# Interleaved linear and softmax attention on one core: squares of VectorE's exponentials go to GpSimd, and the passage between the attentions is reordered

## The chip, the cores and the metric

The kernel runs on one core of one Trainium2 chip, as one launch. The metric is the device time of that launch in microseconds (us); lower is better. The engines are named as the profile names them: PE (TensorE, matrix products), ACT (ScalarE), DVE (VectorE), POOL (GpSimd), and SP (SyncE), which issues the transfers.

## The reference

Two blocks, A and B, are applied in turn, A, B, A, B, to x of shape 1 x 2048 x 1024 (32 heads of 32), each behind a layer norm and with a residual addition.

```python
def _A_ref(x, wqkv, w_phi, wo):          # linear attention
    q, k, v = split_heads(x @ wqkv)
    pq, pk = q @ w_phi, k @ w_phi        # per head
    phi_q = concat(softmax(pq), softmax(-pq))
    phi_k = concat(softmax(pk), softmax(-pk))
    kv, z = phi_k^T @ v, sum(phi_k)
    o = (phi_q @ kv) / (phi_q @ z + 1e-6)
    return merge_heads(o) @ wo

def _B_ref(x, wqkv, wo):                 # softmax attention
    q, k, v = split_heads(x @ wqkv)
    p = softmax(q @ k^T * 32 ** -0.5)
    return merge_heads(p @ v) @ wo

x = x + _A_ref(layernorm(x)); x = x + _B_ref(layernorm(x))
x = x + _A_ref(layernorm(x)); x = x + _B_ref(layernorm(x))
```

## The kernel before

x stays in SBUF as `xR` (16 row tiles of 128 x 1024). Four chunks of 512 rows are worked on. A "layer" is one A block and the B block behind it, so there are two. For each, the A block's keys and values are made chunk by chunk (`a_keys`), summed into a state (`a_state`), and read by the queries (`a_queries`, `a_out`); then comes the softmax attention (`attention`), whose output projection (`b_out`) adds into `xR`. In the first layer, the next layer's norms and keys of chunks 0 to 2 are made beside the attention; only those of chunk 3 have to wait for its end.

Nothing is issued in the order in which it is written. The functions record operations with a planned length, a priority and buffers. `Sched.run` then plays a model of the five engines, takes the ready operation of lowest priority number on each, grants buffers, and writes the instructions in the order it finds. Each engine on the chip runs its instructions strictly in that order and waits for semaphores where data or buffers are not there yet. All SBUF buffers come from one arena of 162 KB per partition; PSUM's eight banks are granted by class, with quotas (`QUOTA`).

**The attention.** A unit is 128 keys x 512 queries of one head: 2048 units a layer. PE makes the scores of up to three units into one half of banks 0 to 5 (L1148), ACT takes the exponential of all of them in one instruction (L1208), and PE multiplies the result by the values and by ones into bank 6 (L1337), which DVE copies out (L1353). Bank 7 is for the projections that run beside it (L544, in four column groups), whose results DVE copies out (L994, L1006, L1022). DVE also computes some exponentials itself (`exp_dve`), of units `spare` picks some 34 units ahead, two to a `pair`. L1290 clamps the scores from PSUM to SBUF as fp32 `y` (class `xy`, two buffers in the tile `work`); then follows a chain on `y` and on `x` (class `xx`, one buffer in `work`). In the first layer each unit goes through by itself (128 x 512):

- mask the mantissa of `y` into `x` (L1111), mask the exponent of `y` (L1114);
- `v`: y = (x + R) * y (L1098);
- `h`: x = (x + B) * x (L1098), the square;
- last: e = (x + C) * y, to bf16 in the arena (L1098).

In the second layer both units of a pair go together (128 x 1024), and the result comes as two bf16 factors whose products are summed by PE:

```python
m = ts(... scalar1=0x007FFFFF, scalar2=0x3F000000 ...)   # L1102: mask y into x
a = ts(... scalar1=0x7F80, scalar2=EXP2S_D ...)          # L1105: high half of y to e2
h = stt(x_v, x_v, EXP2S_B, x_v, a, [x_b])                # L1098: x = (x + B) * x
done.append(stt(e_v, x_v, EXP2S_C, y_v, h, [x_b, y_b, e_b], 0.12))
```

All of the chain is on DVE. POOL only makes constants, clears (L836, L1409) and one small cast per key tile (L779).

**The end of the first attention.** `b_out` multiplies the last chunk's outputs by the projection in two steps: six eighths early, into `part`, the last two when the last heads are there (banks `TAIL`). Eight additions (L1062), two for each row tile, write `xR`. `ln_rows` then does the statistics (L580, L583), ACT the root (L598, L601), DVE the scaling (L607), PE the transposition (L617), ACT the copy (L620), and the key products begin (L540).

**Dummy products.** While an attention is open, `Sched.run` puts a product into a throw-away bank (`idle`, `idle_acc`) where the model shows PE with less than `KEEP` = 0.75 of the last 3.4 us at work. Outside of the attentions there are none.

Of the kernel before, what the change touches and what calls it, by code (L numbers as in the profile page):

```python
# [21 lines left out]
C512 = 512  # L22

# [37 lines left out]
class Sched:  # L61
    def __init__(self, sbuf_bytes, quota):
        self.ops = []
        self.quota = quota
        self.live = {}
        self.free = [(0, sbuf_bytes)]
        self.bank_used = [False] * 11
# [128 lines left out]
    def run(self):  # L196
# [21 lines left out]
        accum = False  # L218
        started = {}
        for o in self.ops:  # L220
            if o.ndep == 0:
                heapq.heappush(ready[o.eng], (0 if o.first else 2, o.prio, o.seq, o))
        t, left, order = 0.0, len(self.ops), []
        while left:
            moved = False
            for e in engines:
                if busy[e] > t + 1e-9 or not ready[e]:
                    continue
# [23 lines left out]
                for s in skipped:  # L252
                    heapq.heappush(ready[e], s)
                if pick is None and e == "PE" and self.idle is not None and self.live.get("S", 0):
# [19 lines left out]
                if pick.hook is not None:  # L274
                    pick.hook(pick)
                    left += self.more
                    self.more = 0
                if e == "PE":
                    recent.append((t, t + pick.dur))
                    if pick.accum is not None:  # L280
                        accum = pick.accum
                d = pick.dur
                if pick.mode is not None:
# [45 lines left out]

SBUF_ARENA = 162 * 1024  # L330
WIDE = 3
# [4 lines left out]
MODEST = {"slabk", "xn1", "e1", "vp1", "pkf", "wo", "bo"}  # L336
QUOTA = {"pk": 3, "pv": 3, "kv": 1, "mm": 4, "cmp": 5, "bc": 6, "num": 1, "wt": 5, "wx": 2, "fil": 3,
         "e": 6, "vp": 6, "e1": 4, "vp1": 4, "E": 10, "q2": 4, "kt": 4, "w2": 5, "oT": 27, "T": 4, "den": 2,
         "eq": 8, "ns": 4, "cw": 6, "hl": 6, "oc": 2, "slab": 12, "slabk": 3, "fin": 4,
         "rs": 8, "pkf": 1, "cden": 2, "part": 8, "w2r": 1,  # L340
         "wo": 1, "st": 4, "xo": 6, "bn": 4, "xs": 1, "xy": 5, "xx": 1, "E1": 5}
CORE = {"E", "E1", "T", "den", "cden", "oT"}
E_SIZE = 3 * 1024
HOLES = 3
SPELL = 3.4
KEEP = 0.75

ONE = 2.0**23
# [55 lines left out]
WIRE = 360.0  # L404
BACKLOG = 1.0
KV_MM = 0.042


@with_exitstack
def kernel(  # L410
# [59 lines left out]
    arena = arena_p.tile([P, ARENA // 2], BF16, tag="arena")  # L470
    work = const.tile([P, 3, 2 * C512], F32, tag="work")
    psum = psum_p.tile([P, 8 * C512], F32, tag="psum")
# [523 lines left out]
    def soon(o):  # L996
        o.first = True
        return o
# [49 lines left out]

    def b_out(t, fc, c, prio, w, oT, banks, last, part=None, lo=0, hi=4):

        wb, ww, wd = w
        pb, pv = ps("fil", banks)
        ts = slice(t * P, (t + 1) * P)
# [7 lines left out]
        def add(out_, in0, deps, bufs):  # L1061
            return soon(op("DVE", dve_us(512), lambda: nc.vector.tensor_tensor(  # L1062
                out=out_(), in0=in0(), in1=pv(), op=ALU.add), [m, *deps], [pb, *bufs], prio))
        x_v = lambda: xR[:, row, fs]
# [17 lines left out]
    def exp_dve(pair, prio, each):  # L1082

        n = len(pair["got"])
        y_b, e_b = pair["bufs"]
        x_b, x = fixed("xx", [(10,)])
        sch.enter(x_b, prio)
        done = []
        for lo, hi in [(k, k + 1) for k in range(n)] if each else [(0, n)]:
# [7 lines left out]
            def stt(out_, in0, scalar, in1, dep, bufs, us=0.0):  # L1097
                return sch.later("DVE", dve_us(w * 512) + us, lambda: nc.vector.scalar_tensor_tensor(  # L1098
                    out=out_(), in0=in0(), scalar=scalar, in1=in1(), op0=ALU.add, op1=ALU.mult), [dep], bufs, prio)
            got = done[-1:] + pair["got"][lo:hi]  # L1100
            if pair["split"]:
                m = ts(lambda y_v=y_v, x_v=x_v: nc.vector.tensor_scalar(  # L1102
# [19 lines left out]
    def attention(base, kT, vT, q_of, gate, most, mix, turns, pos, split, ahead, near, load, each):  # L1122

# [130 lines left out]
        def spare(rows, turn, more):  # L1254
# [10 lines left out]
            if pair is None:  # L1265
                y_b, y_v = fixed("xy", [(8,), (9,)])
                e_b, e_v = sb("E1", 4 if split else 2, C512)
                new += [y_b, e_b]
# [6 lines left out]
            if pair is None:  # L1275
                state["pair"] = {"split": split, "got": [], "units": [], "y": y_v, "e": e_v, "bufs": (y_b, e_b),
                                 "flat": lambda: e_v().rearrange("p a b -> p (a b)")}
                for b in (y_b, e_b):
                    b.left += 1
# [147 lines left out]
    for layer in range(2):  # L1427
# [87 lines left out]
        oTs = attention(at, kT, vT, q_of, gate, MOST[layer], MIX[layer], turns, pos, SPLIT[layer], AHEAD[layer], NEAR[layer], LOAD[layer], EACH[layer])  # L1515
        if last:
# [28 lines left out]
        for i in range(G):  # L1545
# [63 lines left out]
```

## Time and profile before

| what | us |
|---|---|
| median of 3 runs | 2268.9 (2268.39 to 2270.06) |
| the profiled execution | 2269.66 |
| its span, first to last instruction | 2267.9 |
| PE busy | 2192.6 |
| ACT busy | 1997.2 |
| DVE busy | 1892.7 |
| POOL busy | 26.9 |

The span is what lies between the first and the last instruction; the execution's own time is 1.8 us longer. A busy PE is not PE at its peak, since matrix products are pipelined and their ends are modelled. A row of a group gives line, engine, operation, out<-in, shapes and count, then busy us and mean ns, then idle us before it and what ended that. A row of a timeline gives start and length in us.

### The profile page before, as it was taken

How to read it: one execution, taken by the hardware profiler on the slowest of the kernel's cores; microseconds unless marked ns; L12 is line 12 of the kernel's file. 1: busy time of each engine (PE TensorE's matmuls, PEld its weight loads, DVE VectorE, ACT ScalarE, POOL GpSimd, SP SyncE). 2: the span in 40 equal slices, each digit the busy share in tenths (PEclk: the TensorE clock that was granted, in tenths of full speed). 3: DMA queues.
4: the chain of work that ended last, by engine and by line, in shares of the span. 5: the costliest groups of instructions: out<-in, count | busy, mean ns of one | idle time of the engine just before them, and what ended most of it. 6: DMA issues, size and time to landing. Idle time of an engine off the chain costs nothing.

```text
span 2267.9 us, 65202 instructions
## 1 busy us (share of the span) xinstructions
PE 2192.6 (97%) x28080; PEld 823.7 (36%) x28080; DVE 1892.7 (83%) x3015; ACT 1997.2 (88%) x1970; POOL 26.9 (1%) x78
## 2 busy tenths in 40 slices
PE   9999999999999999999998999999999999999998
PEld 5543443333333333333333444443333333333332
DVE  8866536999899999999897686357999899899997
ACT  6447669999999999999896644899999999999998
POOL 1000000000000000000000000000000000000000
PEclk9999999999999999999999999999999999999999
DMA  8701221111223314314344013111111111121111
GB/s 234 202 5 38 71 59 28 44 48 47 61 77 90 100 54 120 89 54 132 114 118 124 1 38 100 36 35 29 40 39 38 44 37 38 37 73 51 46 30 35
DMA packets 235193, 150.56 MB, mean 66 GB/s; under 512 B 131608, under 2 KB 211480, under 8 KB 234904
## 3 DMA queue, kind: packets, MB, share of 16 engines
q1 hardware_dynamic: 234904, 146.40, 23.4%
q8 instruction: 219, 3.59, 0.6%
q14 instruction: 70, 0.57, 0.1%
HBM read 81.59 MB, written 27.77 MB: 48 GB/s over the span
## 4 chain that ended last, share of the span: by engine, by line
PE 51%; ACT 30%; DVE 9%; issue 7%; DMA 2%; SPq 1%; ACTq 0%; POOL 0%; DVEq 0%; POOLq 0%
ACT arena L1208 27%; PE psum L540 14%; PE psum L544 14%; PE psum L1337 11%; PE psum L1148 9%; DVE work L1098 1%; DVE work L1290 1%; DVE arena L1098 1%; DMA arena<-in_B_wo_dram 1%; DVE arena L953 1%; DMA arena<-rd 1%; DVE arena L765 1%; PE psum L796 1%; DVE xR L968 1%; ACT arena L935 1%
## 5 line engine op out<-in xcount | busy, mean ns | idle before, releaser
L1208 ACT ACTIVATE arena<-psum 128x1536 bf16<-128x1536 f32 (+1 forms) x1337 | 1673.0, 1422 | 13.2 <-PE psum L1148 11.2
L1337 PE MATMUL psum<-arena 128*32 128x512 bf16 x4328 | 663.3, 383 | 2.5 <-DVE arena L1353 2.1
L1337 PE MATMUL psum<-arena,ones_bf 128*32 128x512 bf16 x4328 | 663.9, 383 | 1.7 <-issue 1.7
L544 PE MATMUL psum<-arena 128*32 128x512 bf16 (+1 forms) x8768 | 613.6, 377 | 8.7 <-DVE arena L757 2.0
L1148 PE MATMUL psum<-arena 32*128 32x512 bf16 x4096 | 523.6, 384 | 42.4 <-ACT arena L1208 36.7
L540 PE MATMUL psum<-arena 128*128 128x512 bf16 (+1 forms) x2032 | 451.0, 374 | 4.6 <-DVE arena L1374 2.2
L1098 DVE SCALAR_TENSOR_TENSOR work<-work 128x512 f32<-128x512 f32 (+1 forms) x456 | 374.8, 822 | 8.1
L1148 PEld LDWEIGHTS <-arena 32*128 32x128 bf16 x4096 | 153.9, 91 | 579.4 <-issue 571.7
L1290 DVE TENSOR_SCALAR work<-psum 128x512 int32<-128x512 f32 x402 | 275.3, 686 | 62.7 <-PE psum L1148 58.9
L544 PEld LDWEIGHTS <-arena 128*32 128x32 bf16 x8768 | 197.5, 96 | 253.5 <-issue 145.3
L540 PEld LDWEIGHTS <-arena 128*128 128x128 bf16 x2032 | 192.6, 98 | 231.1 <-issue 23.2
L1337 PEld LDWEIGHTS <-arena 128*32 128x32 bf16 x4328 | 186.3, 95 | 237.4 <-issue 156.1
L1098 DVE SCALAR_TENSOR_TENSOR arena<-work 128x512 bf16<-128x512 f32 (+1 forms) x286 | 257.3, 900 | 4.9
L1337 PEld LDWEIGHTS <-ones_bf 128*32 128x32 bf16 x4328 | 185.3, 95 | 30.2 <-issue 8.8
L994 DVE CAST arena<-psum 128x512 bf16<-128x512 f32 (+1 forms) x104 | 67.2, 646 | 55.4 <-PE psum L544 54.7
L761 ACT ACTIVATE arena<-psum 128x512 bf16<-128x512 f32 x80 | 43.4, 594 | 73.0 <-PE psum L540 64.0
L893 ACT ACTIVATE arena<-psum 128x512 bf16<-128x512 f32 x128 | 70.7, 597 | 40.0 <-PE psum L540 37.6
L765 DVE TENSOR_REDUCE arena<-arena 128x32 f32<-128x1024 bf16 x64 | 77.8, 1215 | 21.1 <-ACT arena L761 19.3
L1353 DVE COPY arena<-psum 128x512 f32<-128x512 f32 x126 | 86.0, 683 | 9.5 <-PE psum L1337 9.3
L544 PE MATMUL psum<-xR,onesD 128*32 128x512 bf16 x1148 | 89.7, 380 | 0.4 <-DVE work L1290 0.2
L1102 DVE TENSOR_SCALAR work<-work 128x1024 int32<-128x1024 int32 x116 | 79.9, 689 | 2.6
L774 DVE TENSOR_TENSOR arena<-psum,arena 128x1024 bf16<-128x1024 f32 x64 | 77.5, 1212 | 4.2 <-DVE arena L768 0.2
(98 smaller groups left out, 1272.4 us busy)
## 6 DMA issues: line engine op xcount, KB each, us to landing
arena<-rd SPq DMA_DIRECT2D x62, 256.0 KB
arena<-in_B_wqkv_dram SPq DMA_DIRECT2D x51, 256.0 KB
xa<-arena SPq DMA_DIRECT2D x48, 256.0 KB
arena<-in_A_wqkv_dram SPq DMA_DIRECT2D x40, 256.0 KB
arena<-in_B_wo_dram SPq DMA_DIRECT2D x40, 256.0 KB
arena<-arena SPq DMA_DIRECT2D x256, 32.0 KB
arena<-wd_k SPq DMA_DIRECT2D x32, 256.0 KB
arena<-arena SPq DMA_DIRECT2D x62, 128.0 KB
```

The lines of the kernel that those rows point to most:

```text
L540: nc.tensor.matmul(out_, lhsT=lhsT, rhs=rhs, start=start, stop=stop, skip_group_check=True)
L544: nc.tensor.matmul(out_[ks, :], lhsT=lhsT[:, ks], rhs=rhs, start=start, stop=stop, tile_position=(0, 32 * k), skip_group_check=True)
L765: red = op("DVE", dve_us(1024), lambda ev=ev, sv=sv: nc.vector.reduce_sum(out=sv(), in_=ev().rearrange("p s (h d) -> p (s h) d", d=DH), ax ...
L774: ml = op("DVE", dve_us(1024), lambda vpv=vpv, wv_=wv_, sv=sv: nc.vector.tensor_tensor(out=wv_()[:, :, :, 0:DH], in0=vpv().rearrange("p (h ...
L893: ex = [op("ACT", act_us(512), lambda s=s, pv=pv, ev=ev: nc.scalar.activation(out=ev()[:, s, :], in_=pv(), func=ACT.Exp, scale=(1.0, -1.0) ...
L1098: return sch.later("DVE", dve_us(w * 512) + us, lambda: nc.vector.scalar_tensor_tensor(out=out_(), in0=in0(), scalar=scalar, in1=in1(), op ...
L1102: m = ts(lambda y_v=y_v, x_v=x_v: nc.vector.tensor_scalar(out=x_v().bitcast(I32), in0=y_v().bitcast(I32), scalar1=0x007FFFFF, scalar2=0x3F ...
L1148: nc.tensor.matmul(out=out_, lhsT=kT[g][1]()[r, pp, d * P:(d + 1) * P], rhs=q_of[(qc, g)][1]()[r, (pp + j // 2) % 2, :], start=True, stop= ...
L1208: ex = make("ACT", act_us(w * C512), lambda: nc.scalar.activation(out=e_v()[:, 0:w * C512], in_=s_v()[:, 0:w * C512], func=ACT.Exp, scale= ...
L1290: pair["got"].append(sch.later("DVE", dve_us(512) + 0.13, lambda: nc.vector.tensor_scalar(out=y_v().bitcast(I32)[:, k, :], in0=s_v(), scal ...
L1337: nc.tensor.matmul(out=a_v()[col:col + 32, :], lhsT=v_v()[:, kc % 4, o:o + DH] if what == 0 else ones_bf[:], rhs=ev()[:, x * C512:(x + 1) ...
L1353: cp = op("DVE", dve_us(512), lambda t_v=t_v, a_v=a_v: nc.vector.tensor_copy(out=t_v(), in_=a_v()), [last], [a_b, t_b], prio - 4)
```

## The change

1. The square goes to POOL in both layers (`HALF_POOL`), as two instructions in place: x = x + B/2, then x = x * x. The last step's constant takes up the difference. In the second layer POOL is released by L1102's mask, in the first by `v`; the last step on DVE waits for POOL. `x` gets a second buffer (`XS`), for which the arena gives up 4 KB per partition. The scheduler's model is told `POOL_NS` = 2.87 ns per element for the product and 0.9 for the shift.
2. The last chunk's additions in the first layer get the priority of the norm that reads them, tile by tile, instead of coming ahead of everything; the tail products get a class of banks of their own (`tl`).
3. Outside of the attentions, behind the first 40 us of the model, dummy products (`idle_at`) are put into a free bank where the model shows PE at work for less than 0.95 of the last 3.4 us. The model now also counts a product at double length for 4 us after PE was idle for 2.1 of the last 3.4 us.

```diff
+YS, XS = 2, 2
...
+                if pick is None and e == "PE" and self.idle is not None and not self.live.get("S", 0) and t > WARM_UP:
+                    recent = [r for r in recent if r[1] > t - SPELL]
+                    spot = next((x for x in (7, 5, 4, 3, 2, 1, 0) if not self.bank_used[x]), None)
+                    if sum(not x for x in self.bank_used[:8]) > 1 and sum(r[1] - max(r[0], t - SPELL) for r in recent) < KEEP_N * SPELL:
+                        pick = Op("PE", MM, 0.0, lambda spot=spot: self.idle_at(spot), (Buf("ps", 0, "idle", [(spot,)]),), 0.0, "n", 0)
...
+                    if t > WARM_UP and sum(r[1] - max(r[0], t - SPELL) for r in recent) < SPELL - REST:
+                        slow = t + DIP
+                    if t < slow:
+                        d *= 2
...
-SBUF_ARENA = 162 * 1024
+SBUF_ARENA = (162 - 4 * (YS + XS - 3)) * 1024
...
+KEEP_N = 0.95
+REST = 2.1
+DIP = 4.0
+WARM_UP = 40.0
...
+POOL_NS = 2.87
+HALF_POOL = (True, True)
...
-        pb, pv = ps("fil", banks)
+        pb, pv = ps("tl" if banks is TAIL else "fil", banks)
...
-            return soon(op("DVE", dve_us(512), lambda: nc.vector.tensor_tensor(
-                out=out_(), in0=in0(), in1=pv(), op=ALU.add), [m, *deps], [pb, *bufs], prio))
+            o = op("DVE", dve_us(512), lambda: nc.vector.tensor_tensor(
+                out=out_(), in0=in0(), in1=pv(), op=ALU.add), [m, *deps], [pb, *bufs], prio if add_at is None else add_at)
+            return o if add_at is not None else soon(o)
...
-        x_b, x = fixed("xx", [(10,)])
+        x_b, x = fixed("xx", [(8 + YS + i,) for i in range(XS)])
...
+            def square(scalar, dep):
+                if not pair["pool"]:
+                    return stt(x_v, x_v, scalar, x_v, dep, [x_b])
+                sh = sch.later("POOL", w * C512 * 0.9 / 1000 + 0.1, lambda x_v=x_v: nc.gpsimd.tensor_scalar(
+                    out=x_v(), in0=x_v(), scalar1=scalar / 2, scalar2=None, op0=ALU.add), [dep], [x_b], prio)
+                return sch.later("POOL", w * C512 * POOL_NS / 1000 + 0.1, lambda x_v=x_v: nc.gpsimd.tensor_tensor(
+                    out=x_v(), in0=x_v(), in1=x_v(), op=ALU.mult), [sh], [x_b], prio)
...
-                h = stt(x_v, x_v, EXP2S_B, x_v, a, [x_b])
-                done.append(stt(e_v, x_v, EXP2S_C, y_v, h, [x_b, y_b, e_b], 0.12))
+                h = square(EXP2S_B, m if pair["pool"] else a)
+                done.append(stt(e_v, x_v, EXP2S_C - (EXP2S_B**2 / 4 if pair["pool"] else 0.0), y_v, [h, a], [x_b, y_b, e_b], 0.12))
...
-            h = stt(x_v, x_v, EXP2_B, x_v, v, [x_b])
-            done.append(stt(e_v, x_v, EXP2_C, y_v, h, [x_b, y_b, e_b], 0.12))
+            h = square(EXP2_B, v)
+            done.append(stt(e_v, x_v, EXP2_C - (EXP2_B**2 / 4 if pair["pool"] else 0.0), y_v, h, [x_b, y_b, e_b], 0.12))
...
-                new[qc][t].append(b_out(t, fc, qc, pr, w, oTs[qc], TAIL, last, part, 3, 4))
+                new[qc][t].append(b_out(t, fc, qc, pr, w, oTs[qc], TAIL, last, part, 3, 4,
+                                        BASE[1] + 10 * qc - LA + 0.01 * t - 0.005))
...
+    def idle_at(x):
+        nc.tensor.matmul(psum[:, x * C512:(x + 1) * C512], lhsT=onesD[:], rhs=xR[:, 0, 0:C512], start=True, stop=True)
+    sch.idle_at = idle_at
```

More of the change, by code (lines that the diff above doesn't have):

```diff
@@ L66, in __init__ @@
         self.free = [(0, sbuf_bytes)]
-        self.bank_used = [False] * 11
+        self.bank_used = [False] * 14
         self.peak = 0
@@ L219, in run @@
         started = {}
+        slow = 0.0
         for o in self.ops:
@@ L226, in run @@
             for e in engines:
-                if busy[e] > t + 1e-9 or not ready[e]:
+                if busy[e] > t + 1e-9 or not ready[e] and (e != "PE" or t < WARM_UP):
                     continue
@@ L253, in run @@
                     heapq.heappush(ready[e], s)
+                if pick is None and e == "PE" and self.idle is not None and not self.live.get("S", 0) and t > WARM_UP:
[3 more added lines that the diff above has]
+                        pick = Op("PE", MM, 0.0, lambda spot=spot: self.idle_at(spot), (Buf("ps", 0, "idle", [(spot,)]),), 0.0, "n", 0)
+                        pick.bufs[0].left, pick.late = 1, True
+                        self.queue["idle"] = [list(pick.bufs), 0]
+                        assert self._alloc(pick.bufs)
+                        left += 1
                 if pick is None and e == "PE" and self.idle is not None and self.live.get("S", 0):
@@ L470 @@
     arena = arena_p.tile([P, ARENA // 2], BF16, tag="arena")
-    work = const.tile([P, 3, 2 * C512], F32, tag="work")
+    work = const.tile([P, YS + XS, 2 * C512], F32, tag="work")
     psum = psum_p.tile([P, 8 * C512], F32, tag="psum")
@@ L1047, in b_v, with b_out @@
             done[(t, h)] = e
-    def b_out(t, fc, c, prio, w, oT, banks, last, part=None, lo=0, hi=4):
+    def b_out(t, fc, c, prio, w, oT, banks, last, part=None, lo=0, hi=4, add_at=None):
         wb, ww, wd = w
-        pb, pv = ps("fil", banks)
+        pb, pv = ps("tl" if banks is TAIL else "fil", banks)
         ts = slice(t * P, (t + 1) * P)
@@ L1098, in stt @@
                 return sch.later("DVE", dve_us(w * 512) + us, lambda: nc.vector.scalar_tensor_tensor(
-                    out=out_(), in0=in0(), scalar=scalar, in1=in1(), op0=ALU.add, op1=ALU.mult), [dep], bufs, prio)
+                    out=out_(), in0=in0(), scalar=scalar, in1=in1(), op0=ALU.add, op1=ALU.mult), dep if isinstance(dep, list) else [dep], bufs, prio)
             got = done[-1:] + pair["got"][lo:hi]
+            def square(scalar, dep):
[5 more added lines that the diff above has]
+                    out=x_v(), in0=x_v(), in1=x_v(), op=ALU.mult), [sh], [x_b], prio)
             if pair["split"]:
@@ L1117, in exp_dve, with attention @@
             v = stt(y_v, x_v, EXP2_R, y_v, a, [x_b, y_b])
-            h = stt(x_v, x_v, EXP2_B, x_v, v, [x_b])
-            done.append(stt(e_v, x_v, EXP2_C, y_v, h, [x_b, y_b, e_b], 0.12))
+            h = square(EXP2_B, v)
+            done.append(stt(e_v, x_v, EXP2_C - (EXP2_B**2 / 4 if pair["pool"] else 0.0), y_v, h, [x_b, y_b, e_b], 0.12))
         return done
-    def attention(base, kT, vT, q_of, gate, most, mix, turns, pos, split, ahead, near, load, each):
+    def attention(base, kT, vT, q_of, gate, most, mix, turns, pos, split, ahead, near, load, each, pool):
         units = [
@@ L1265, in spare @@
             if pair is None:
-                y_b, y_v = fixed("xy", [(8,), (9,)])
+                y_b, y_v = fixed("xy", [(8 + i,) for i in range(YS)])
                 e_b, e_v = sb("E1", 4 if split else 2, C512)
@@ L1275, in spare @@
             if pair is None:
-                state["pair"] = {"split": split, "got": [], "units": [], "y": y_v, "e": e_v, "bufs": (y_b, e_b),
+                state["pair"] = {"split": split, "pool": pool, "got": [], "units": [], "y": y_v, "e": e_v, "bufs": (y_b, e_b),
                                  "flat": lambda: e_v().rearrange("p a b -> p (a b)")}
@@ L1514 @@
                     q_of[(qc, g)] = q_back(g, qc, at + 10 * pos[(qc, g)] - QB, away)
-        oTs = attention(at, kT, vT, q_of, gate, MOST[layer], MIX[layer], turns, pos, SPLIT[layer], AHEAD[layer], NEAR[layer], LOAD[layer], EACH[layer])
+        oTs = attention(at, kT, vT, q_of, gate, MOST[layer], MIX[layer], turns, pos, SPLIT[layer], AHEAD[layer], NEAR[layer], LOAD[layer], EACH[layer], HALF_POOL[layer])
         if last:
```

9 lines of the change are left out of this document (5 added, 4 removed).

## The prediction

> **What bounds the kernel now.** I read the page first, then busy time by stage, then the groups with their shapes kept apart.
>
> ```profile
> PE 2192.6 (97%) x28080; PEld 823.7 (36%) x28080; DVE 1892.7 (83%) x3015; ACT 1997.2 (88%) x1970; POOL 26.9 (1%) x78
> ```
>
> The shares mix stages, so I asked for busy time in four stretches: the first layer's attention, the passage to the second layer, the projections after it, the second layer's attention. Columns: stretch, length, then busy time of PE, PEld, DVE, ACT, POOL, granted clock, DMA share, GB/s.
>
> ```profile
> 350.00:1216.00 866.00, 830.65 (x12370) 286.82 (x12371) 805.04 (x1401) 855.77 (x715) 9.99 (x25) 0.99 0.29 81
> 1216.00:1236.00 20.00, 14.22 (x101) 6.75 (x94) 14.00 (x27) 7.21 (x16) 0.00 (x0) 0.83 0.53 172
> 1236.00:1444.00 208.00, 206.50 (x1506) 93.53 (x1508) 140.16 (x240) 108.62 (x199) 2.59 (x8) 1.00 0.17 46
> 1444.00:2262.00 818.00, 796.01 (x11052) 273.70 (x11053) 702.71 (x951) 809.93 (x657) 0.00 (x0) 1.00 0.14 39
> ```
>
> The two attentions are 866 + 818 = 1684 us of the 2267.9 us span. ScalarE is busy for 99% of both (855.77 of 866, 809.93 of 818): its exponentials set the pace. VectorE follows with 93% and 86%; GpSimd does nothing worth naming. What ScalarE waits for in the two attentions (engine, line, releaser, us, times, longest):
>
> ```profile
> ACT arena L1208 <- PE psum L1148: 7.3, 9, 3.3
> ACT arena L1208 <- PE psum L1148: 3.8, 11, 0.6
> ```
>
> So a lighter VectorE alone can give back about 11 us, unless it takes exponentials off ScalarE.
>
> **Part 1: does VectorE take more exponentials?** In the built order VectorE converts 398 units instead of 402 (170 single in the first attention as before, 228 in pairs instead of 232), and ScalarE gets 1024 three-wide and 313 two-wide instructions.
>
> ```profile
> L1208 ACT ACTIVATE arena<-psum 128x1536 bf16<-128x1536 f32 x1021 | 1432.9, 1522 | 10.1 <-PE psum L1148 8.5 <-PE psum L1337 0.5 <-ACT arena L1208 0.2
> 1179.71 29.55 ACT L1208 ACTIVATE arena<-psum 128x1536 bf16<-128x1536 f32 x23
> ```
>
> 23 three-wide ones in a row take 29.55 us, 0.43 us per unit, so four more units cost ScalarE +1.7 us. Nothing comes off the engine that bounds; the offload frees only VectorE.
>
> **Part 2: what leaves VectorE.** The square `h` (L1098, in place in `work`); its neighbours in the chain, and the copies that share its engine:
>
> ```profile
> L1098 DVE SCALAR_TENSOR_TENSOR work<-work 128x512 f32<-128x512 f32 x340 | 233.8, 688 | 8.1
> L1098 DVE SCALAR_TENSOR_TENSOR work<-work 128x1024 f32<-128x1024 f32 x116 | 141.1, 1216 | 0.0
> L1098 DVE SCALAR_TENSOR_TENSOR arena<-work 128x1024 bf16<-128x1024 f32 x116 | 140.4, 1210 | 0.8
> L1102 DVE TENSOR_SCALAR work<-work 128x1024 int32<-128x1024 int32 x116 | 79.9, 689 | 2.6
> L1105 DVE TENSOR_SCALAR arena<-work 128x1024 uint16<-128x1024 uint16 x116 | 79.3, 684 | 0.0
> L1396 DVE TENSOR_TENSOR arena<-arena 128x512 bf16<-128x512 f32 x62 | 42.4, 684 | 4.6 <-DMA arena<-rd 2.7 <-DMA arena<-arena 0.9 <-PE psum L1148 0.5
> ```
>
> Half of the 340 go: 170 x 0.688 = 117 us in the first attention, and 116 x 1.216 = 141 us in the second. Left for VectorE: 805 - 117 = 688 us, 4.05 per unit (170 units, one every 866/170 = 5.09 us), and 703 - 141 = 562 us, 4.93 per pair (114 pairs, one every 818/114 = 7.18 us).
>
> **Part 3: what GpSimd costs.** The trace has no arithmetic of this size on GpSimd. Its nearest rows:
>
> ```profile
> L779 POOL CAST arena<-arena 128x32 bf16<-128x32 f32 x64 | 21.1, 330 | 1230.8 <-DMA xd<-arena 627.5 <-DVE arena L768 457.6 <-DMA arena<-rd 88.8
> L836 POOL MEMSET arena<- 128x2048 bf16 x2 | 3.6, 1810 | 5.2 <-ACT arena L1208 5.2
> L1409 POOL MEMSET arena<- 128x1024 bf16 x1 | 1.0, 951 | 0.0
> ```
>
> The memsets give (1810 - 951)/1024 = 0.84 ns per element, the cast 0.33 us for almost nothing. Estimate of the shift (one input): 0.33 + 480 x 0.84 ns = 0.73 us at 512, 0.33 + 992 x 0.84 ns = 1.16 us at 1024. The product reads twice. Below, it costs what the shift does (0.73, 1.16); above, three passes in turn (two reads, a write): 0.33 + 480 x 2.52 ns = 1.54 and 2.83 us. I take two and a half passes, 1.34 and 2.4, since reads in turn are the likelier. With 0.2 us for the passing of a signal (below, the cast starts 0.22 us behind the reciprocal that releases it), GpSimd needs 2.3 us per unit (1.6 to 2.5) and 3.8 us per pair (2.5 to 4.2). The Trainium skill, GPSIMD Engine Reference, section Elementwise — side-by-side cycle accounting, puts a two-input operation at about 2.6 cycles of 1.2 GHz per element; as an estimate that is 1.1 and 2.2 us and a fixed part, near the value taken, and the sum would be the same.
>
> **Part 4: what it costs VectorE.** This decides. Two places of the trace show both engines at once (start, length):
>
> ```profile
> 1160.01 1.81 POOL L836 MEMSET arena<- 128x2048 bf16 x1 [5.18 <-ACT arena L1208]
> 1160.52 1.58 DVE L1111 TENSOR_SCALAR work<-work 128x512 int32<-128x512 int32 x1
> L1111 DVE TENSOR_SCALAR work<-work 128x512 int32<-128x512 int32 x170 | 71.7, 422 | 1.2
> ```
>
> ```profile
> 955.64 0.35 DVE L768 RECIPROCAL arena<-arena 128x32 f32<-128x32 f32 x1
> 955.91 0.63 DVE L1098 SCALAR_TENSOR_TENSOR work<-work 128x512 f32<-128x512 f32 x1
> 956.21 0.50 POOL L779 CAST arena<-arena 128x32 bf16<-128x32 f32 x1 [13.32 <-DVE arena L768]
> ```
>
> An L1111 that takes 0.42 us elsewhere takes 1.58 us when it meets a memset on GpSimd: it ends 0.28 us behind the memset's end at 1161.82, so it stood still for it. And a cast beside an L1098 takes 0.50 instead of 0.33. So the two exclude each other, both ways, in just the forms this chain is made of. The Trainium skill, SBUF — State Buffer, section Who interferes with whom, states this as a rule that speaks against the change: VectorE in a two-port mode, or with two SBUF inputs, and GpSimd share one port pair, held for a whole instruction. The trace agrees: 1.58 us against 0.42.
>
> Then GpSimd's time and VectorE's locking work (both masks, the product `v`, the last step, L1396) add up, and only VectorE's reads of PSUM (the clamp L1290, copies) run beside GpSimd. Without any overlap a unit needs 4.05 + 2.3 = 6.35 us and has 5.09; a pair needs 4.93 + 3.8 = 8.73 us and has 7.18. VectorE's reads of PSUM start 0.6 us apart:
>
> ```profile
> 1192.27 0.69 DVE L1062 TENSOR_TENSOR arena<-xR,psum 128x512 f32<-128x512 bf16 x1
> 1192.88 0.68 DVE L1290 TENSOR_SCALAR work<-psum 128x512 int32<-128x512 f32 x1
> 1193.48 0.68 DVE L1353 COPY arena<-psum 128x512 f32<-128x512 f32 x1
> ```
>
> The built order tells the overlap: between what starts GpSimd and the step that waits for it stand on average 2.2 non-locking VectorE instructions (first attention) and 2.75 (second): 1.34 and 1.65 us. But in 152 of 170 units and 99 of 114 pairs a locking one stands there too, and what is behind it can't pass. With all of the overlap: 5.01 of 5.09 and 7.08 of 7.18, 98% and 99% full. With 85% of it (my choice): 6.35 - 1.14 = 5.21 and 8.73 - 1.40 = 7.33, over the pace by 0.12 x 170 = 20 us and 0.15 x 114 = 17 us. VectorE becomes the bound by a little: **+37 us**. What is queued behind a VectorE instruction that stands still is the clamp that frees a score bank and the copies that free banks 6 and 7, for which TensorE waits, and then ScalarE.
>
> Also on GpSimd: 24 casts L779 in the first attention now queue behind squares, up to 2.3 us each; they feed key products planned later, so I put them at 0 (without that cover, 6 accumulations x 2.3 = 14 us).
>
> **Part 5: between the attentions.** Here the change gains.
>
> ```profile
> 1218.91 4.29 PE L540 MATMUL psum<-arena 128*128 128x512 bf16 x15 [0.41 <-DVE arena L1374]
> 1219.49 4.86 DVE L1062 TENSOR_TENSOR xR<-arena,psum 128x512 bf16<-128x512 f32 x8
> 1224.28 1.27 DVE L580 BATCH_NORM_STATS2 arena<-xR 128x6 f32<-128x512 bf16 x2
> 1231.01 2.77 PE L540 MATMUL psum<-arena 128*128 128x512 bf16 x6
> ```
>
> The first statistics wait for all eight additions (4.86 us). In the new order they wait for two (1.2 us): 3.6 us earlier, and the chain to the first key product with them; later tiles arrive one per 3.2 us of VectorE against 16 key and value products (3.5 us), so TensorE is not starved. And six products take 2.77 us where 15 took 4.29: the clock had dropped (0.83 in this stretch). 17 dummy products in the gap hold it up: 20 us x 0.17 = 3.4 us of clock, some 2.4 of it in useful work. Together **-6 us**. The other 31 dummies stand in gaps that the plan sees (26 in the tail, 5 among the projections); a planned gap that isn't there costs at most 31 x 0.22 = 7 us, I take 0. The arena is 4 KB smaller and seven banks for the tail replace three: 0, the loads they delay being covered by ScalarE's pace.
>
> **Sum.** The profiled execution took 2269.66 us, 0.8 over the median 2268.9. 2269.7 + 1.7 + 37 - 6 = **2302 us**. What a measurement can tell from no change is 0.2%, 4.5 us.
>
> **Rivals.**
> 1. *The squares hide* (0.30). The product costs its lower bound and overlap is full: 4.93 + 2.5 - 1.65 = 5.8 of 7.18, 4.05 + 1.6 - 1.34 = 4.3 of 5.09. VectorE has slack, half of ScalarE's 11 us of waits goes, the passage gains 6: 2269.7 + 1.7 - 6 - 6 = 2259 us. For it: ScalarE kept 99% with VectorE at 93%. It decides where GpSimd's pair stays under 3.5 us.
> 2. *Gain and loss cancel* (0.09): stalls of 5 us against the passage's 6 give 2269.
> 3. *Heavy exclusion* (0.10): three passes and half of the overlap: 4.93 + 4.2 - 0.83 = 8.3 and 4.05 + 2.5 - 0.67 = 5.9, over the pace by 1.1 x 114 + 0.8 x 170 = 260 us. GpSimd catches up while VectorE waits for products, so I count half: 2269 + 130 = about 2400 us.
> 4. *The step that waits is late, not VectorE* (0.04): GpSimd always loses the lock, results miss their products by 1 us in a quarter of 284 cases, 71 us, 2335.
>
> **How the numbers follow.** The forecast (0.47) is 2302, its own range 2275 to 2345 (overlap from 95% to 70%, product from two passes to three). The range over all cases, 2255 to 2390, takes in most of rival 1 and leaves out its best end (0.07), and the far end of rival 3 (0.06). Faster by over 0.2% is rival 1, 0.30; within it rival 2, 0.09; slower the forecast with rivals 3 and 4, 0.61.
>
> **What would show it.** The masks L1111 and L1102 (L1144 and L1135 in the new code) longer than 422 and 689 ns on average; GpSimd busy for 25 to 50% of both attentions; VectorE's busy time, stalls included, over 95% there; ScalarE waiting for score products (L1181) for tens of us instead of 11; first statistics two additions after the last TAIL product. Wrong if the masks keep their 0.42 and 0.69 us, or if ScalarE's waits stay near 11 us: then rival 1 holds.

## The result, and the profile after

The changed kernel takes 2408.6 us (median of 4, 2406.06 to 2410.12) against 2268.9 us: ratio 1.062, 95% interval 1.060 to 1.063, or 140 us slower. Forecast were 2302 us, with a range up to 2390.

The page's first part, of the changed kernel:

```profile
PE 2242.7 (93%) x28107; PEld 825.7 (34%) x28168; DVE 1815.8 (75%) x2719; ACT 2021.9 (84%) x1970; POOL 1063.0 (44%) x646
```

VectorE is 77 us less busy than before, where 117 + 141 = 258 us of squares have gone: its other work has become longer. Busy time by stage (length, then PE, PEld, DVE, ACT, POOL, clock): first attention, passage, projections, second attention:

```profile
350.00:1271.00 921.00, 847.71 (x12351) 287.11 (x12351) 757.21 (x1229) 865.56 (x714) 459.63 (x365) 0.98 0.27 75
1271.00:1284.00 13.00, 12.79 (x106) 5.95 (x100) 10.88 (x21) 4.00 (x8) 0.00 (x0) 1.00 0.84 245
1284.00:1483.00 199.00, 196.36 (x1349) 91.27 (x1370) 140.96 (x244) 100.22 (x197) 2.59 (x8) 1.00 0.20 55
1483.00:2398.00 915.00, 837.10 (x11238) 276.25 (x11237) 673.07 (x823) 834.26 (x663) 586.42 (x228) 0.98 0.13 35
```

By the exponentials' rows in the timeline, the last one of the first attention ends at 1270.9 us, before at 1216.2: 55 us later. The second attention lasts from 1483.4 to 2397.7, before from 1433.6 to 2257.2: 91 us longer. Between the first attention's last exponential and the first of the keys lie 13.5 us for 17.6. ScalarE, busy for 99% of both attentions before, is at 94% and 91%. The clock granted to TensorE is 0.98 in both, where it was 0.99 and 1.00; whether that carries a part of the loss or only follows from TensorE's idle time isn't taken apart. What the engines wait for (ScalarE's exponentials, then VectorE's last step, over the whole kernel):

```profile
ACT arena L1241 <- PE psum L1181: 84.0, 125, 2.8
ACT arena L1241 <- PE psum L1370: 36.3, 46, 3.8
```

```profile
DVE arena L1123 <- POOL work L1132: 178.7, 133, 4.0
```

Here ScalarE's exponentials wait for TensorE for 120 us; before it was 12 (11.2 for the scores, 0.7 for the products with the values). VectorE stands for 179 us before its last step because the square isn't there. The groups of GpSimd, shift (L1130) and product (L1132); the mean of one is behind the second comma:

```profile
L1130 POOL TENSOR_SCALAR work<-work 128x1024 f32<-128x1024 f32 x114 | 358.5, 3144 | 477.1 <-DVE work L1135 474.8
L1130 POOL TENSOR_SCALAR work<-work 128x512 f32<-128x512 f32 x170 | 269.4, 1585 | 591.8 <-DVE work L1123 591.8
L1132 POOL TENSOR_TENSOR work<-work 128x1024 f32<-128x1024 f32 x114 | 228.0, 2000 | 9.5
L1132 POOL TENSOR_TENSOR work<-work 128x512 f32<-128x512 f32 x170 | 180.8, 1064 | 14.2
```

A unit costs GpSimd 1.585 + 1.064 = 2.65 us and a pair 5.14 us, where 2.1 and 3.6 were taken (the prediction's 2.3 and 3.8 hold 0.2 us for a signal). And VectorE's groups, of which the masks stood at 422 and 689 ns, the second mask of a pair at 684, the last step at 688 and 1210, the clamp at 686:

```profile
L1123 DVE SCALAR_TENSOR_TENSOR arena<-work 128x1024 bf16<-128x1024 f32 x114 | 160.4, 1407 | 95.7 <-POOL work L1132 95.2
L1138 DVE TENSOR_SCALAR arena<-work 128x1024 uint16<-128x1024 uint16 x114 | 130.6, 1145 | 0.0
L1135 DVE TENSOR_SCALAR work<-work 128x1024 int32<-128x1024 int32 x114 | 103.8, 911 | 2.8
L1144 DVE TENSOR_SCALAR work<-work 128x512 int32<-128x512 int32 x170 | 88.9, 523 | 1.8
L1323 DVE TENSOR_SCALAR work<-psum 128x512 int32<-128x512 f32 x398 | 271.7, 684 | 105.0 <-PE psum L1181 89.4 <-ACT arena L1241 7.7 <-issue 5.7
```

All of the chain's steps that work in SBUF got longer (those not shown too: the second mask of a unit from 424 to 574 ns, `v` and a unit's last step from 688 to 751 and 745); the clamp L1323, which reads PSUM, did not. How one such stall travels shows in the timeline of the second attention (start, length):

```profile
1898.88 0.69 DVE L1135 TENSOR_SCALAR work<-work 128x1024 int32<-128x1024 int32 x1
1898.92 2.40 POOL L1132 TENSOR_TENSOR work<-work 128x1024 f32<-128x1024 f32 x1
1899.49 2.38 DVE L1138 TENSOR_SCALAR arena<-work 128x1024 uint16<-128x1024 uint16 x1
1901.41 3.09 POOL L1130 TENSOR_SCALAR work<-work 128x1024 f32<-128x1024 f32 x1
1901.80 2.05 DVE L1123 SCALAR_TENSOR_TENSOR arena<-work 128x1024 bf16<-128x1024 f32 x1
1903.77 0.68 DVE L1386 COPY arena<-psum 128x512 f32<-128x512 f32 x1
1904.50 0.38 PE L1370 MATMUL psum<-arena 128*32 128x512 bf16 x1 [2.14 <-DVE arena L1386]
1905.21 3.95 ACT L1241 ACTIVATE arena<-psum 128x1536 bf16<-128x1536 f32 x3 [2.21 <-PE psum L1370]
```

L1138 meets a product and takes 2.38 instead of 0.68 us: it ends 0.55 us behind the product, so it stood still for it. L1123 meets the next shift and takes 2.05 instead of 1.21. The copy L1386 behind them comes late, TensorE stands for 2.14 us on it, and ScalarE for 2.21 us.

### The profile page after: what moved, and what is told of

Read it like the earlier page. It is cut to its first block, busy times and chain, and to the rows that moved or that the text cites. A ratio compares the mean times of both kernels' runs of the same rounds, so it can differ in the third digit from the quotient of the medians.

```text
span 2408.3 us, 65673 instructions
## 1 busy us (share of the span) xinstructions
PE 2242.7 (93%) x28107; PEld 825.7 (34%) x28168; DVE 1815.8 (75%) x2719; ACT 2021.9 (84%) x1970; POOL 1063.0 (44%) x646
## 5 line engine op out<-in xcount | busy, mean ns | idle before, releaser
L1241 ACT ACTIVATE arena<-psum 128x1536 bf16<-128x1536 f32 (+1 forms) x1337 | 1696.5, 1376 | 132.3 <-PE psum L1181 84.0
L1130 POOL TENSOR_SCALAR work<-work 128x512 f32<-128x512 f32 (+1 forms) x284 | 627.9, 2211 | 1068.9 <-DVE work L1123 591.8
L1181 PE MATMUL psum<-arena 32*128 32x512 bf16 x4096 | 546.8, 389 | 52.5 <-ACT arena L1241 24.9
L1123 DVE SCALAR_TENSOR_TENSOR arena<-work 128x512 bf16<-128x512 f32 (+1 forms) x284 | 286.9, 1010 | 179.5 <-POOL work L1132 178.7
L1132 POOL TENSOR_TENSOR work<-work 128x512 f32<-128x512 f32 (+1 forms) x284 | 408.8, 1439 | 23.7
L1323 DVE TENSOR_SCALAR work<-psum 128x512 int32<-128x512 f32 x398 | 271.7, 684 | 105.0 <-PE psum L1181 89.4
L1138 DVE TENSOR_SCALAR arena<-work 128x1024 uint16<-128x1024 uint16 x114 | 130.6, 1145 | 0.0
L1123 DVE SCALAR_TENSOR_TENSOR work<-work 128x512 f32<-128x512 f32 x170 | 127.2, 751 | 4.3
L803 POOL CAST arena<-arena 128x32 bf16<-128x32 f32 x64 | 22.3, 348 | 229.7 <-DVE arena L792 176.0
L1135 DVE TENSOR_SCALAR work<-work 128x1024 int32<-128x1024 int32 x114 | 103.8, 911 | 2.8
L917 ACT ACTIVATE arena<-psum 128x512 bf16<-128x512 f32 x128 | 70.7, 597 | 40.3 <-PE psum L564 32.6
```

Of the source, the lines that this page charges most:

```text
L917: ex = [op("ACT", act_us(512), lambda s=s, pv=pv, ev=ev: nc.scalar.activation(out=ev()[:, s, :], in_=pv(), func=ACT.Exp, scale=(1.0, -1.0) ...
L1130: sh = sch.later("POOL", w * C512 * 0.9 / 1000 + 0.1, lambda x_v=x_v: nc.gpsimd.tensor_scalar(out=x_v(), in0=x_v(), scalar1=scalar / 2, sc ...
L1132: return sch.later("POOL", w * C512 * POOL_NS / 1000 + 0.1, lambda x_v=x_v: nc.gpsimd.tensor_tensor(out=x_v(), in0=x_v(), in1=x_v(), op=AL ...
L1135: m = ts(lambda y_v=y_v, x_v=x_v: nc.vector.tensor_scalar(out=x_v().bitcast(I32), in0=y_v().bitcast(I32), scalar1=0x007FFFFF, scalar2=0x3F ...
L1138: a = ts(lambda y_v=y_v, e2_v=e2_v: nc.vector.tensor_scalar(out=e2_v().bitcast(U16), in0=high(y_v()), scalar1=0x7F80, scalar2=EXP2S_D, op0 ...
L1181: nc.tensor.matmul(out=out_, lhsT=kT[g][1]()[r, pp, d * P:(d + 1) * P], rhs=q_of[(qc, g)][1]()[r, (pp + j // 2) % 2, :], start=True, stop= ...
```

## Experiments

Three theories stood at the outset. First: GpSimd's shift is far slower than reckoned, squares come late, and VectorE stands in order before the last step. Second: GpSimd blocks VectorE's SBUF operations, and what is queued behind them is late. Third: the order was written for other durations. Each run was timed against the kernel before on the same chip (2267 to 2269 us). "VectorE" is its busy time plus the waits of its last step for GpSimd in the profiled execution.

| run | us | ratio to before, interval | VectorE, us |
|---|---|---|---|
| the change | 2408.6 | 1.0617 (1.0603 to 1.0632) | 1816 + 179 |
| shift_as_two_inputs | 2380.1 | 1.0504 (1.0488 to 1.0520) | 1877 + 70 |
| squares_second_layer | 2378.5 | 1.0491 (1.0476 to 1.0505) | 1889 + 98 |
| nobody_waits | 2351.7 | 1.0371 (1.0357 to 1.0385) | 1879 + 0 |
| true_durations | 2346.2 | 1.0356 (1.0332 to 1.0380) | 1805 + 114 |
| squares_first_layer | 2323.7 | 1.0248 (1.0234 to 1.0262) | 1838 + 83 |
| square_in_order_place | 2311.0 | 1.0193 (1.0179 to 1.0207) | 1884 + 0 |
| plan_knows_stalls | 2288.8 | 1.0095 (1.0081 to 1.0109) | 1736 + 101 |
| no_shift | 2288.6 | 1.0093 (1.0077 to 1.0110) | 1769 + 8 |
| three_quarter_width | 2282.9 | 1.0071 (1.0057 to 1.0084) | 1742 + 64 |
| no_product | 2268.4 | 1.0007 (0.9998 to 1.0017) | 1705 + 17 |
| half_width | 2266.8 | 0.9996 (0.9987 to 1.0005) | 1689 + 20 |
| no_early_additions | 2265.8 | 0.9990 (0.9981 to 0.9999) | 1886 + 0 |
| narrow_squares | 2263.1 | 0.9983 (0.9974 to 0.9993) | 1648 + 4 |
| all_on_vectore | 2261.2 | 0.9971 (0.9959 to 0.9982) | 1887 + 0 |
| no_gap_dummies | 2260.5 | 0.9968 (0.9957 to 0.9979) | 1886 + 0 |

**Which part of the change.** The square back on VectorE, the passage as changed:

```diff
-YS, XS = 2, 2
+YS, XS = 2, 1
-HALF_POOL = (True, True)
+HALF_POOL = (False, False)
```

> Both layers keep the square on VectorE (one multiply-add there, as before); the passage's additions, the dummy products and the clock account stay as changed, one squares buffer instead of two. First theory (GpSimd's shift takes 1.49 and 2.77 us where 0.73 and 1.16 were reckoned, the squares come late, and VectorE stands in order before the step that needs them) and second theory (GpSimd's operations block VectorE's, which take longer): the whole loss lies in the squares, so this runs at 2263 to 2266 us, the passage's 4 us and a little less than before's 2268.9. If the other edits share in the loss, over 2270 us.

2261.2 us: 0.3% faster than before, and 2 us below the range expected. All of the loss is in the squares. Then layer by layer, `(True, False)`, and `(False, True)` with an arena of 157 KB:

> Squares on GpSimd in the first layer's attention alone (170 single units). The attention was 55 us longer in the changed kernel. Both theories: 2265 + 55 = about 2320 us. Third theory (the order written for wrong durations couples the two attentions, so that a delay in the first spoils the second): more than 2335 us.

> Squares on GpSimd in the second layer's attention alone (114 pairs), the arena 1 KB smaller. That attention was 91 us longer in the changed kernel. Both theories: 2265 + 90 = about 2355 us; third theory: much less, under 2330 us, since no delay comes in from the first attention.

2323.7 is 62 us above all_on_vectore and near what was expected; 2378.5 is 117 above it and 23 more than expected. In the second the passage, which has no squares, holds a stall (ScalarE's wait, us, times, longest; in all_on_vectore these are 27.9, 10 and 5.8):

```profile
ACT arena L622 <- DVE arena L607: 48.4, 10, 25.6
```

So the attentions themselves are the better measure, by the exponentials' rows in the timelines. With squares in the first layer alone the first attention ends 57 us later than in all_on_vectore (1269.8 for 1213.1), with both 58 us. With squares in the second layer alone the second attention lasts 916.1 us for 826.6, 89 us longer, with both 914.3, 88 us longer. The layers add up, and no delay passes from one to the other; the third theory's form with a coupling falls.

**Wait or blocking.** The waits go, GpSimd's work stays:

```diff
-  last step: (x_v + constant) * y_v, behind h
+  last step: (y_v + constant) * y_v     (x_v unread)
```

> The same order on every engine and the same operations on GpSimd, but VectorE's last step reads the exponent's tile twice instead of the square (so the softmax weights are other numbers): nobody waits for GpSimd, and it still works beside VectorE. First theory (late squares, 178.7 us of waits): most of the loss goes, 2265 to 2300 us. Second theory (blocking alone): the masks stay long and the time stays at 2370 to 2410 us.

Neither: 57 us go, and 89 of the 145 us above narrow_squares stay. The first theory, which put nearly all on lateness, falls; both mechanisms are at work.

Then the two operations one by one (the other isn't issued), and both cut to 32, to 256 and to 384 of 512 columns:

```diff
-  out=x_v(), in0=x_v()
+  out=x_v()[:, :, 0:32], in0=x_v()[:, :, 0:32]     (in1 likewise; 0:256; 0:384)
```

> The same order, GpSimd makes the product alone and leaves the shift out (the exponentials' polynomial is then wrong). GpSimd's work per unit falls from 2.65 to 1.1 us, per pair from 5.1 to 2.0 us. First theory (the shift is the term that makes the squares late): 2265 to 2295 us. Second theory (the product is what blocks VectorE: an L1144 that starts inside one takes 1.07 instead of 0.42 us): the loss stays for the most part, over 2340 us.

> The same order, GpSimd makes the shift alone and leaves the product out (the polynomial is then wrong). GpSimd's work per unit falls to 1.5 us, per pair to 2.9 us. First theory: part of the lateness stays, 2285 to 2330 us. Second theory (only the product blocks fully): nearly all of the loss goes, under 2280 us.

> The same order and the same waits, but the shift and the product take 32 columns of each 512 (the other columns stay unsquared). Both theories: GpSimd's time goes and with it the loss, 2255 to 2270 us. If the passing of signals between the engines, or the place of the last step in VectorE's order, is what costs: over 2300 us.

no_shift lost 25 us against narrow_squares and no_product 5, both together 145. no_shift lies in the first theory's range and no_product in the second's, and neither had foreseen that the parts don't add up. narrow_squares came out as both expected: signals and order alone cost hardly anything, and nothing is won either (2263.1 against all_on_vectore's 2261.2), although VectorE has 239 us less to do. The widths show where the loss begins:

> The same order and waits, shift and product on the first 256 of each 512 columns (the others stay unsquared). If the loss is in proportion to GpSimd's work, half of the 145 us between narrow_squares and the change: about 2336 us. If VectorE's freed time takes up the first part of it, as no_shift (25 us) and no_product (5 us) against 145 us for both speak for: 2268 to 2295 us.

> The same order and waits, shift and product on 384 of each 512 columns (the others stay unsquared), between half_width (2267 us) and the change (2409 us). If the loss grows in proportion beyond half: 2338 us. If there is a point up to which the freed time of VectorE covers it, and the loss then speeds up: 2285 to 2315 us. By VectorE's occupied time (busy and waiting for GpSimd: 1,709 us at half, 1,995 us at full width, 1,850 between them, where no_shift with 1,777 lost 25 us): about 2305 us.

2263, 2267, 2283, 2409 us from a sixteenth, a half, three quarters and all of the columns: flat, then steep. The half and the three quarters lie 1 and 2 us below the ranges that slack in VectorE had led to expect. GpSimd's groups in three_quarter_width:

```profile
L1130 POOL TENSOR_SCALAR work<-work 128x768 f32<-128x768 f32 x114 | 281.6, 2470 | 528.0 <-DVE work L1135 527.6
L1130 POOL TENSOR_SCALAR work<-work 128x384 f32<-128x384 f32 x170 | 217.4, 1279 | 621.6 <-DVE work L1123 621.6
L1132 POOL TENSOR_TENSOR work<-work 128x768 f32<-128x768 f32 x114 | 170.8, 1499 | 9.5
L1132 POOL TENSOR_TENSOR work<-work 128x384 f32<-128x384 f32 x170 | 148.3, 873 | 14.2
```

That is 2.15 us per unit and 3.97 per pair, with 0.2 us for a signal 2.35 and 4.17: for a unit nearly the prediction's 2.3, for a pair near its upper end, 4.2. The loss over narrow_squares is 20 us there. The plan, too, reckons with 2.13 and 4.06 us for shift and product together (0.56 + 1.57, 1.02 + 3.04). So the curve turns up where GpSimd becomes slower than planned, and that may be its reason as well as the end of VectorE's slack; the widths don't tell the two apart.

**Load or order.** The order of the change, GpSimd idle, and VectorE's own multiply-add straight ahead of the last step:

```diff
-  GpSimd: shift, product
+  VectorE, ahead of the last step: x = (x + B) * x
```

> The order written for the changed kernel, GpSimd left idle: VectorE makes the square itself, as one multiply-add straight ahead of the last step (170 x 0.69 + 114 x 1.22 = 256 us of work that the order doesn't reckon with). VectorE is then as busy as in nobody_waits (about 1,880 us), but nothing waits for GpSimd and nothing is blocked. If mere load on VectorE that the plan didn't reckon with costs the time, 2340 to 2360 us as in nobody_waits; if it is the blocking, with single operations held for 1 to 2 us at places that the plan thinks short, 2262 to 2285 us.

Between both: 48 us over narrow_squares. VectorE is as busy as in all_on_vectore and nobody_waits:

```profile
PE 2211.9 (96%) x28107; PEld 824.3 (36%) x28168; DVE 1883.5 (82%) x3003; ACT 2012.2 (87%) x1970; POOL 27.8 (1%) x78
```

2261 us with that load in the plan, 2311 with it unplanned and unblocked, 2352 in the form of stalls. So the 145 us between narrow_squares and the change divide, by taking away one after another and rounded, into 57 for waits, 41 for the load coming as stalls, and 48 for load that the order doesn't know of. Another sequence could divide them otherwise, and the 41 hold a difference of place too: in square_in_order_place all of the load lies ahead of the last step, the stalls lie at the masks as well.

The other way round, the plan is told the truth, first on GpSimd alone:

```diff
-  "POOL", w * C512 * 0.9 / 1000 + 0.1          (shift)
+  "POOL", w * C512 * 2.5 / 1000 + 0.2
-  "POOL", w * C512 * POOL_NS / 1000 + 0.1      (product)
+  "POOL", w * C512 * 1.66 / 1000 + 0.2
```

> The same operations, the plan told what GpSimd takes: 1.48 and 2.76 us for the shift (planned 0.56 and 1.02), 1.05 and 1.9 us for the product (planned 1.57 and 3.04), so that the waiting step is written later in VectorE's order. If the misplaced order is the cause: under 2310 us. If blocking and the sum of both engines' work are: 2370 us or more. First theory says 2320 to 2360 us, since the plan then gives VectorE fewer exponentials or places them later.

2346, within the first theory's range and 62 us better, with 386 units on VectorE for 398. Then (shift + 0.3) with VectorE's lengthened operations too:

```diff
+EX = (0.11, 0.15, 0.07, 0.06, 0.22, 0.46, 0.20)    # added to the planned time of each
```

> As true_durations, and the plan also reckons with VectorE's operations as long as the changed kernel's profile has them (L1144 0.11 us longer than planned, L1147 0.15, the product v 0.07, the last step 0.06; in pairs the masks 0.22 and 0.46 and the last step 0.20). If a load is harmless when the order is written for it, as in all_on_vectore (VectorE busy for 1,887 us, 2261 us) against square_in_order_place (1,884 us, 2311 us): clearly under true_durations' 2346, 2290 to 2330 us. If blocking falls on other places as soon as the order changes, so that no plan of mean lengths helps: 2340 to 2360 us.

2288.8: 120 of the 140 us are gone, with the same two instructions on GpSimd. ScalarE's exponentials and its waits in this run:

```profile
L1242 ACT ACTIVATE arena<-psum 128x1536 bf16<-128x1536 f32 x1059 | 1472.2, 1513 | 12.8 <-PE psum L1182 5.6 <-PE psum L1371 2.6 <-PE psum L568 1.8
L1242 ACT ACTIVATE arena<-psum 128x1024 bf16<-128x1024 f32 x277 | 299.6, 1081 | 3.9 <-PE psum L1182 2.1 <-PE psum L1371 1.6
```

ScalarE waits hardly more than before the change. About half of the 28 us left over all_on_vectore's 2261 is its own work: the plan gives VectorE 365 units (the clamp's count) for 398, and 33 x 0.43 us (the prediction's price of a unit on ScalarE) are 14 us. So the third theory, without the coupling, carries a good part of the loss: an order that doesn't know of stalls and late squares. How large a part isn't told apart, since with 33 units fewer GpSimd works for 946 us on squares instead of 1037. An estimate from the widths: between three quarters and all of the columns GpSimd's time goes from 818 to 1037 us and the kernel's by 126, so that an even share would give 91/219 x 126 = 52 of the 120 us to the lighter load, and leave 68 to the order.

**The shift's form.**

```diff
-  tensor_scalar(out=x, in0=x, scalar1=B / 2, op0=add)
+  tensor_tensor(out=x, in0=x, in1=<column of B / 2, repeated>, op=add)
```

> The same order; the shift is a two-input addition of a constant from SBUF (one column read again and again) instead of an addition of an immediate. If it runs as the product does, 1.04 and 1.89 us instead of 1.49 and 2.77, GpSimd's part falls to 2.2 and 3.9 us. First theory (duration and lateness): 2340 to 2375 us. Second theory (blocking; the two-input form blocks fully, the shift now only in part): no gain or a loss, 2395 to 2440 us.

28 us better than the change, 5 us above the first theory's range and below the second's, clearly a gain:

```profile
L1133 POOL TENSOR_TENSOR work<-work,hb 128x1024 f32<-128x1024 f32 x114 | 252.6, 2215 | 527.6 <-DVE work L1138 527.6
L1133 POOL TENSOR_TENSOR work<-work,hb 128x512 f32<-128x512 f32 x170 | 196.2, 1154 | 633.4 <-DVE work L1126 633.4
L1126 DVE SCALAR_TENSOR_TENSOR arena<-work 128x1024 bf16<-128x1024 f32 x114 | 194.1, 1703 | 24.7 <-POOL work L1135 24.6
```

The shift with two inputs takes 1.15 and 2.22 us where the one with one input takes 1.59 and 3.14. The waits for GpSimd fall from 179 to 70 us, while the last step of a pair becomes longer (1407 to 1703 ns): a part of the waits turned into blocking.

**The passage.** From all_on_vectore, once the additions' priority and once the dummies are taken back:

```diff
-  BASE[1] + 10 * qc - LA + 0.01 * t - 0.005      (add_at)
+  None
```

> As all_on_vectore, without the early places of the passage's additions (each has its batch's own place as before). If the 4 us of the passage come from the additions: 2265 to 2268 us; if they come from the dummy products' clock: 2261 us as all_on_vectore.

```diff
-if pick is None and e == "PE" and self.idle is not None and ... t > WARM_UP:
+if False:
```

> As all_on_vectore (2261.2 us), without the dummy products in the gaps outside the attentions; the early additions stay. no_early_additions gave 2265.8, so the additions carry 4.6 of the 6.6 us. If the dummies carry the rest: 2263 to 2264 us; if they do nothing or cost something: 2259 to 2262 us.

Without the early additions 4.6 us are lost; without the dummies nothing is. In the stretch from 1216 to 1236 us the clock is whole without them:

```profile
1216.00:1236.00 20.00, 17.92 (x105) 8.73 (x104) 18.98 (x32) 9.76 (x20) 0.97 (x3) 1.00 0.44 155
```

The last exponential ends at 1211.9 us in this run, and from 1212 to 1216 the clock is 1.00 too. TensorE's longest idle stretch in the passage is 1.8 us, where it was 4.2. So the tighter passage by itself keeps the clock up. Another 1.8 us (2267.7 to 2265.8, with an interval that nearly reaches no change) belong to what the other runs share with no_early_additions. There, with the dummies and without the early additions, the clock is whole as well, and from the first attention's last exponential to the second's first one it takes 204.2 us for 207.5 before. So alone the dummies, or the plan's new clock account, may be worth something; beside the early additions they aren't. That isn't divided further.

## Why the prediction was wrong, point by point

**Part 1** holds: 398 units on VectorE, 1024 three-wide and 313 two-wide exponentials on ScalarE.

**Part 2** holds about in its sizes (narrow_squares: VectorE 244 us lighter than before, for 258), and so does the sentence that a lighter VectorE alone can give little: 2263.1.

**Part 3 is the term that was mis-sized.** The product was rated too high (1.34 and 2.4 us against 1.06 and 2.00) and the shift less than half of what it is (0.73 and 1.16 against 1.59 and 3.14); together 2.65 and 5.14 us, beyond the upper ends given, 2.5 and 4.2, even without the 0.2 us for a signal that these hold. GpSimd was busy for 50% and 64% of the two attentions, where 25 to 50% had been named. The shift was priced by a memset and a small cast, neither of which does arithmetic. The undisturbed ones in the timeline are 1.49 and 2.77 us for the shift, 1.04 and 1.89 for the product: 2.5 and 1.66 ns per added element. With GpSimd's time near what Part 3 took, the chip gave 2283 us (three_quarter_width), within the forecast's own range of 2275 to 2345. The Trainium skill, GPSIMD Engine Reference, section Elementwise — side-by-side cycle accounting, gives some 2.6 cycles of 1.2 GHz per element for two inputs, as an estimate 2.2 ns; the product here is faster than that, with 1.66 ns. The section lays its figure to two reads that take turns, by which the form with one input would be the faster one; here it is the slower. The measurement decides.

**Part 4** named the right mechanism, blocking, and the right carriers: masks longer, reads of PSUM not, TensorE and then ScalarE short of what is queued behind. But **its sum failed too**: it set VectorE's load against the pace, in which nothing is lost until VectorE is full. VectorE was not full: 757 + 84 us of waits in 921, 91%; 673 + 95 in 915, 84%; over 95% had been expected. The time is lost before that: a stall of 1 to 2 us delays the copy and the clamp behind it in a fixed order, as the timeline of the second attention shows in one place. Some 1,885 us of work on VectorE cost nothing where the order had been written for them (all_on_vectore) and 48 us where it had not. Full exclusion is also too strict for the shift: with Part 4's formula the measured 2.65 and 5.14, and 0.2 for a signal, would give 0.67 x 170 + 1.69 x 114 = 307 us, and the loss over narrow_squares was 145. At three quarters of the width (2.35 and 4.17) it would give 0.17 x 170 + 0.52 x 114 = 88 us, and 20 were lost. So the shift's true price alone would not have given the right time; the two errors lay on opposite sides. The Trainium skill, SBUF — State Buffer, section Who interferes with whom, has the port pair held for a whole instruction. The changed kernel's trace agrees for the product: L1138 above stood for one, and of the 94 steps of the chain that begin inside a product none ends before it. It doesn't for the shift: of 224 steps that begin inside one, 148 end while it still runs. A unit's mask of 0.42 us that begins inside a shift takes at most 0.85, and this one goes through

```profile
602.43 1.49 POOL L1130 TENSOR_SCALAR work<-work 128x512 f32<-128x512 f32 x1 [3.67 <-DVE work L1123]
602.98 0.43 DVE L1144 TENSOR_SCALAR work<-work 128x512 int32<-128x512 int32 x1
```

without any delay.

**Part 5** holds in its sum (-6 us forecast; all_on_vectore is 6.6 below before) but not in its shares: 3.6 us for earlier statistics was 4.6, and the 2.4 us for the dummies' clock was nothing once the earlier statistics were there.

**The rivals.** The hidden squares (2259) come true at a sixteenth of the columns only (2263), and gain and loss cancel at half (2267). The late step was rated at 71 us and a chance of 0.04; nobody_waits puts it at 57 us, not in place of blocking but on top of it. Heavy exclusion (2400, chance 0.10) is next to the result in its time, but by chance: it took GpSimd's unit at 2.5 us and its pair at 4.2, about what three_quarter_width has with a signal (2.35 and 4.17), and that ran 2283. Its capacity sum fails as Part 4's does. The rivals were treated as excluding one another, where the runs show lateness and blocking at work together.

## What to carry to other kernels

An engine that executes an order written ahead can lose time to operations that turn out longer than planned before it is full (here at 84 and 91%). So measure an instruction's duration in its own form and beside its neighbours, and write the order for those numbers, before work is moved. Work moved off an engine that isn't the bound wins little even when it is nearly free: here narrow_squares, at 2263 us, was no faster than the kernel that left the square on VectorE, at 2261. And where a loss comes from two causes, take each away alone and both together, since each alone may seem nearly free, as the shift and the product did here (5 and 25 us alone, 145 together).

## What the runs showed of the hardware

On GpSimd, adding an immediate to f32 in place took 1.49 us at 512 and 2.77 at 1024 columns, where nothing disturbed it, and 1.59 and 3.14 on average. Adding a repeated column from SBUF took 1.03 and 1.89 at the shortest, and 1.15 and 2.22 on average: the form with two inputs is the faster one. A product on GpSimd stopped the chain's steps in SBUF until it ended (94 of 94 that began inside one, in the changed kernel's trace). A shift let 148 of 224 end before it did, with no or part of the delay. VectorE's reciprocals of 128x16 took 0.24 us inside a product as elsewhere, so not all that it does in SBUF is stopped. Why these differ isn't shown.
